# Decode attention and gated FFN, forward and backward: zero stores moved to SP, later loads to ACT, and products cut into pieces between transposes

## The chip, the cores and the metric

The kernel runs on one core of a Trainium2 chip. The metric is the device time of one launch in microseconds (us). The engines are PE (matrix products and transposes; PEld are its weight loads), DVE and ACT (vector and scalar work, and all copies out of the matrix accumulators in PSUM), POOL, and SP, which only issues transfers (DMAs). POOL issues DMAs on one queue (called software_dynamic in the profile), SP and ACT on a hardware queue each (hardware_dynamic). Each engine, and each queue's issuing engine, takes its instructions in order.

## What is computed

The reference is a forward pass and its vector-Jacobian product. Four tokens (B = 4, D = 512) are layer-normed; one branch is grouped-query attention on a cache (32 query heads, 8 K/V heads, head size 128) over the last W = 1024 of 4096 cached positions, the other a gated FFN (F = 1792):

```python
q = (xn @ wq) split into 32 heads
k, v = k_cache[:, :, Sk - W:, :], v_cache[:, :, Sk - W:, :]
p = softmax(q k^T * Dh ** -0.5);  o = p v
out = x + o @ wo + (gelu(xn @ w_gate) * (xn @ w_up)) @ w_down
```

Returned are out and the gradients of x, k_cache, v_cache, wq, wo, w_gate, w_up and w_down for a given grad_out. The gradients of the caches have the caches' full shape, (4, 8, 4096, 128) each, and are zero in the 3072 positions outside the window: these zeros have to be written too. They are 50.3 of the 112.4 MB that the kernel moves.

## The kernel before

Work goes in stages.

- The start (lines 96 to 185): layer norm, transposes of x and grad_out, masked copies `xnm` and `dym`, and a tile of zeros, `ztile`.
- The FFN stage (from 429): `hg_ps` (gate and up products), the activation, transposes of w_down (`wdT_ps`, line 492) with the `da_ps` products, then the weight gradients: `dwd_ps` (529) and `dwg_ps` (542, for gate and up), each copied by `evac` from PSUM into an output tile `osb_d` or `osb_g` and stored; then transposes of the gate and up weights (`wgT_ps`, 555), summed into `acc_ps`.
- Four groups t of two K/V heads (GP = 2, NT = 4). For each: `pre` (225) makes q and do from wq and wo (transposes `woT_ps`, products `doq_ps`); `masks` (262) makes masked copies on POOL; `scores` (271) transposes eight blocks of K (k = 0) or V (k = 1) and multiplies (`T_ps` to `T_sb`, then `S_ps`); `softmax` and `softmax_d`; `odq` (340) the products o (with V) and dq (with K); `dvdk` (364) the gradients dv and dk in 16 products each, copied into a staging tile and stored 1 MB at a time; `fin` (383) sums into out and dx (`acc_ps`, with transposes `wqT_ps`) and makes dwo (`dwo_ps`, 406) and dwq (`dwq_ps`, 418), stored from `osb_o` and `osb_q`.
- The end (592): the sums are transposed (`f_ps`), out and dx are finished and stored.

In the main loop (569) `dvdk(t, 0)`, `scores(t+1, 0)`, `dvdk(t, 1)`, `scores(t+1, 1)` and `fin(t)` follow each other as blocks. SP and POOL take their instructions in program order; PE, DVE and ACT are ordered by a scheduler. PSUM tiles of most products come from one pool of four buffers (`ps_w`), output tiles from one of three (`outp`), staging tiles from one of four. K and V tiles are one batch with two heads each, six buffers per tensor (`kvp`).

SP issues all loads, in the order FFN weights, wo and wq of group 0, K and V of group 0, wo and wq of group 1, K and V of group 1 for two batches; the later ones follow in the loop and wait for a free buffer. POOL issues all stores. The zero stores (`zeros`, 212; 32 of 1.57 MB) stand one by one between the other stores in POOL's order; the first two wait for the last load of group 0's V (line 440). `evac` (82) gives each copy out of PSUM to ACT or DVE, whichever a running sum of estimated costs favours. The memsets of `aT_b`, `dhuT_b` and `dhgT_b` (458) are on POOL.

Of the kernel before, what the change touches and what calls it, by code (L numbers as in the profile page):

```python
# [17 lines left out]
def kernel(  # L18
# [51 lines left out]
    kvp = ctx.enter_context(tc.tile_pool(name="kvp", bufs=6))  # L70
    wres = ctx.enter_context(tc.tile_pool(name="wres", bufs=2))
    attw = ctx.enter_context(tc.tile_pool(name="attw", bufs=2))
    tsb = ctx.enter_context(tc.tile_pool(name="tsb", bufs=3))
# [8 lines left out]
    def evac(out, in_, n, half=False, eng=None):  # L82

        ca, cd = (190 + n) / 1.2, (120 + (n / 2 if half else n)) / 0.96
        if eng is None:
            eng = "act" if load["act"] + ca <= load["dve"] + cd else "dve"
        load[eng] += ca if eng == "act" else cd
        if eng == "act":
            return nc.scalar.copy(out=out, in_=in_)  # L89
        return nc.vector.tensor_copy(out=out, in_=in_)  # L90
# [48 lines left out]
    acc_ps = ps_a.tile([P, 2, ND, B], FP32, name="acc_ps")  # L139

    def acc_edge(start):
        nc.tensor.matmul(acc_ps[:].rearrange("p o c b -> p (o c b)"), lhsT=ztile[0:1, 0:P],
                         rhs=ztile[0:1, 0:2 * ND * B], start=start, stop=not start)

    def acc_add(o, c, lhsT, rhs):
        nc.tensor.matmul(acc_ps[:, o, c, :], lhsT=lhsT, rhs=rhs, start=False, stop=False)  # L146

    acc_edge(True)
    S_ps = ps_a.tile([P, 2, WQ], FP32, name="S_ps")
# [41 lines left out]
    def load_w(t):  # L191
        wo_t[t] = wres.tile([P, HG, D], BF16, name="wo_sb", tag="wo")
        nc.sync.dma_start(out=wo_t[t][:], in_=wo_v[t])  # L193
        wq_t[t] = wres.tile([P, ND, CW], BF16, name="wq_sb", tag="wq")
        nc.sync.dma_start(out=wq_t[t][:], in_=wq_v[t])

    def load_kv(t, bs, which=(0, 1)):
        for i in which:
            d_, src, nm = ((k_t, A_k_cache, "kb"), (v_t, A_v_cache, "vb"))[i]
            for b in bs:  # L200
                tl = kvp.tile([P, GP, J, Dh], BF16, name=nm, tag=nm)
                ld = nc.sync.dma_start(
                    out=tl[:].rearrange("p g j d -> p g (j d)"),
                    in_=src[b, t * GP:(t + 1) * GP, K0:Sk, :].rearrange("g (m j) d -> m g (j d)", j=J))
                d_[(t, b)] = tl
        return ld
# [5 lines left out]
    def zeros(n, after=None):  # L212

        zsrc = bass.AP(tensor=ztile.tensor, offset=ztile.offset, ap=[list(ztile[:].ap[0]), [0, ZG], [1, ZW]])
        for _ in range(min(n, len(zlist))):
            og, b, g = zlist.pop(0)
            z = nc.gpsimd.dma_start(out=og[b, g:g + ZG, 0:K0, :].rearrange("g (m j) d -> m g (j d)", m=P), in_=zsrc)  # L217
            if after is not None:
                tc.add_manual_dep(z.ins, after.ins.name,
                                  mybir.DependencyInfo(mybir.DependencyClass.Sync, mybir.DependencyReason.DATA))  # L220

# [3 lines left out]
    def pre(t):  # L225
# [3 lines left out]
        for h2 in range(HG // 2):  # L229
# [6 lines left out]
            for i in range(2):  # L236
                for c in range(ND):
                    nc.tensor.matmul(dq_ps[:, 0, 2 * h2 + i, :], lhsT=woT[:, i, c, :], rhs=dyT[:, c, :],
                                     start=(c == 0), stop=(c == ND - 1))
        for h in range(HG):  # L240
# [30 lines left out]
    def scores(t, k):  # L271
# [3 lines left out]
        for b in range(B):  # L275
            for g in range(GP):
                T_ps = ps_w.tile([P, J, P], BF16, name="T_ps", tag="w")
                for j in range(J):
                    nc.tensor.transpose(T_ps[:, j, :], blks[(t, b)][:, g, j, :], ident[:])  # L279
# [3 lines left out]
                for q in range(NQ):  # L283
                    nc.tensor.matmul(S_ps[q * RG:(q + 1) * RG, k, :], lhsT=lf[:, s * RG:(s + 1) * RG],  # L284
                                     rhs=T_sb[:, q * WQ:(q + 1) * WQ],
                                     start=(s == 0), stop=(s == NS - 1), tile_position=(0, q * RG))
# [11 lines left out]
    def softmax(t):  # L298
        S = S_ps[:, 0, :]
# [24 lines left out]
    def softmax_d(t):  # L324
        E_f, rr, dP = st[t]["E"], st[t]["rr"], S_ps[:, 1, :]
# [14 lines left out]
    def odq(t, k):  # L340

        pT, blks = st[t][("PT", "dST")[k]], (v_t, k_t)[k]
        for g in range(GP):
            for j in range(J):
                q, jj = j // JQ, j % JQ
                for b in range(B):
                    c0 = q * RG + (b * GP + g) * rep
                    nc.tensor.matmul(od_ps[b * RB:b * RB + rep, k, g, :], lhsT=pT[:, jj, c0:c0 + rep],  # L348
                                     rhs=blks[(t, b)][:, g, j, :], start=(j == 0), stop=(j == J - 1),
# [6 lines left out]
        T_ps = ps_x.tile([P, GP, P], BF16, name="odT_ps", tag="x")  # L356
# [7 lines left out]
    def dvdk(t, k, stage):  # L364
        src, mr, og = ((st[t]["P"], st[t]["do"], out_3), (st[t]["dS"], st[t]["q"], out_2))[k]
        nm = ("dv", "dk")[k]
        for g in range(GP):
            stg = stage.tile([P, B, J, Dh], BF16, name="stg_" + nm, tag="stg")
            for jj in range(JQ):
                for q in range(NQ):  # L370
                    j = q * JQ + jj
                    rs = slice(q * RG, (q + 1) * RG)
                    mps = ps_w.tile([P, B, Dh], FP32, name="kv_ps", tag="w")
                    nc.tensor.matmul(mps[:].rearrange("p b d -> p (b d)"), lhsT=src[rs, jj * P:(jj + 1) * P],  # L374
                                     rhs=mr[rs, g].rearrange("p b d -> p (b d)"), start=True, stop=True,
                                     tile_position=(q * RG, 0))
                    evac(stg[:, :, j, :], mps[:], 512)
            nc.gpsimd.dma_start(  # L378
                out=og[:, t * GP + g, K0:Sk, :].rearrange("b (m j) d -> m b (j d)", j=J),
                in_=stg[:].rearrange("p b j d -> p b (j d)"))  # L380
            zeros(1)

    def fin(t):

        (o_r, oT), (dq_r, dqT) = st[t]["o"], st[t]["dq"]
        wo_sb, wq_sb = wo_t.pop(t), wq_t.pop(t)
        for h in range(HG):
            for c in range(ND):
                acc_add(0, c, wo_sb[:, h, c * P:(c + 1) * P], oT[:, h // rep, h % rep, :])
        for h2 in range(HG // 2):  # L390
# [7 lines left out]
            for i in range(2):  # L398
                h = 2 * h2 + i
                for c in range(ND):  # L400
                    acc_add(1, c, wqT[:, i, c, :], dqT[:, h // rep, h % rep, :])
        for g in range(GP):
            osb = outp.tile([P, rep, D], BF16, name="osb_o", tag="o")
            for i in range(rep):
                mps = ps_w.tile([P, D], FP32, name="dwo_ps", tag="w")
                nc.tensor.matmul(mps[:], lhsT=o_r[:, g, :], rhs=dym[:, i, :], start=True, stop=True)
                evac(osb[:, i, :], mps[:], 512)
            r0 = (t * HG + g * rep) * Dh
            nc.gpsimd.dma_start(out=out_5[r0:r0 + rep * Dh, :].rearrange("(h p) n -> p h n", p=P), in_=osb[:])  # L409
        zeros(1)  # L410
        for c2 in range(ND // 2):
            osb = outp.tile([P, 2, GP, rep, Dh], BF16, name="osb_q", tag="o")
            for ci in range(2):
                c = c2 * 2 + ci
                for i2 in range(rep // 2):
                    mps = ps_w.tile([P, 2, GP, Dh], FP32, name="dwq_ps", tag="w")
                    for i in range(2):
                        nc.tensor.matmul(mps[:, i].rearrange("p g d -> p (g d)"),
                                         lhsT=xnm[:, i2 * 2 + i, c * P:(c + 1) * P],
                                         rhs=dq_r[:].rearrange("p g d -> p (g d)"), start=True, stop=True)  # L420
                    evac(osb[:, ci, :, i2 * 2:(i2 + 1) * 2, :], mps[:].rearrange("p i g d -> p g i d"), 512)
            nc.gpsimd.dma_start(
                out=out_4[c2 * 2 * P:(c2 + 1) * 2 * P, t * CW:(t + 1) * CW].rearrange("(c p) j -> p c j", p=P),
                in_=osb[:].rearrange("p c g i d -> p c (g i d)"))
        zeros(1)
# [3 lines left out]
    with tc.tile_pool(name="ffn_w", bufs=1) as ffn_w, tc.tile_pool(name="ffn", bufs=1) as ffn:  # L429
# [6 lines left out]
        load_w(0)  # L436
        last = load_kv(0, range(B))
        load_w(1)
        load_kv(1, range(2))
        zeros(2, last)  # L440

# [14 lines left out]
        def ftb(name):  # L456
            t_ = ffn.tile([P, 4 * NF4, B], BF16, name=name)
            nc.gpsimd.memset(t_[:], 0.0)
# [49 lines left out]
        for fc in range(NF):  # L508
            for c in range(ND):
                acc_add(0, c, wd_sb[:, fc, c * P:(c + 1) * P], aT_b[:, fc, :])  # L510

        def f_rows(srcT, nm):
# [6 lines left out]
            rows = ffn.tile([P, NF4, P], BF16, name=nm)  # L519
# [3 lines left out]
        a_r = f_rows(aT_b, "a_r")  # L523
        for f4 in range(NF4):
            n = min(4, NF - 4 * f4)
            osb = outp.tile([P, 4, D], BF16, name="osb_d", tag="o")
            for i in range(n):
                mps = ps_w.tile([P, D], FP32, name="dwd_ps", tag="w")
                nc.tensor.matmul(mps[:], lhsT=a_r[:, f4, :], rhs=dym[:, i, :], start=True, stop=True)  # L529
                evac(osb[:, i, :], mps[:], 512)  # L530
            nc.gpsimd.dma_start(out=out_8[4 * f4 * P:(4 * f4 + n) * P, :].rearrange("(h p) n -> p h n", p=P),
                                in_=osb[:, 0:n, :])
            if f4 % 2:
                zeros(1)
# [119 lines left out]
```

## Time and profile before

| | us |
|---|---|
| runs of the kernel | 336.75, 338.77, 339.62 (median 338.77) |
| the profiled execution | 337.38 |
| its span, first to last instruction | 335.5 |
| PE busy in the span | 223.8 (67%) |
| DVE, ACT, POOL busy | 154.4, 127.7, 74.3 |

The mean clock granted to PE was 0.745 of full speed. The transfers moved 112.38 MB (30.93 read, 81.01 written, and a little for instructions), 335 GB/s over the span. In the page, L12 is line 12 of the kernel; `T_ps<-ident,kb` names output and inputs. "Idle before <-" tells what an engine waited for; the chain of waits goes back from the last instruction, at each step to what released it. The slices cut the span in 40 parts; a digit is the busy share in tenths.

### The profile page before, as it was taken

To read this page: it belongs to the slowest core of one execution; us is meant where nothing else is said; L and a number is where in the kernel's file an instruction comes from. 1 tells how busy PE (TensorE), PEld (TensorE's weight loads), DVE (VectorE), ACT (ScalarE), POOL (GpSimd) and SP (SyncE) were. 2 spreads that over 40 slices of the span, in tenths; PEclk is the share of its full clock that TensorE was granted. 3 is DMA by queue.
4 is the path that set the end of the run, shared out by engine and by line. 5 is a ranking of instruction groups with operands and counts; after the bars stand their busy time and mean duration, and the time that the engine had idled before them with its cause. 6 is when DMAs were issued, how large, how long until landed. Compare 5 with 4: busy or idle time off the path is not lost.

```text
span 335.5 us, 6853 instructions
## 1 busy us (share of the span) xinstructions
PE 223.8 (67%) x2956; PEld 142.8 (43%) x2956; DVE 154.4 (46%) x304; ACT 127.7 (38%) x203; POOL 74.3 (22%) x111
## 2 busy tenths in 40 slices
PE   1352182477977899698669689768959988990020
PEld 1352120164856656165346427646542664260010
DVE  6141051336553474456347454534736456870050
ACT  3012041325524363553346354334535347860010
POOL 5000212322140011070313016031201604531010
PEclk9998567559997967679956957795585879576555
DMA  5999999997900079887999999599998938999995
GB/s 175 395 361 385 373 417 418 420 417 312 411 26 2 12 259 380 352 337 301 350 415 418 416 413 410 216 358 416 417 419 347 395 149 325 376 395 403 405 389 211
DMA packets 34661, 112.38 MB, mean 335 GB/s; under 512 B 1920, under 2 KB 8072, under 8 KB 34632
## 3 DMA queue, kind: packets, MB, share of 16 engines
q0 software_dynamic: 16512, 81.01, 59.9%
q1 hardware_dynamic: 18120, 30.94, 26.3%
q8 instruction: 23, 0.38, 0.4%
q14 instruction: 6, 0.05, 0.0%
HBM read 30.93 MB, written 81.01 MB: 334 GB/s over the span
## 4 chain that ended last, share of the span: by engine, by line
PE 50%; DMA 26%; DVE 9%; ACT 5%; SPq 4%; issue 3%; POOL 1%; ACTq 0%; DVEq 0%; POOLq 0%
PE T_ps L279 13%; DMA out_dram<-osb_o 12%; PE kv_ps L374 10%; PE S_ps L284 4%; DMA wq_sb<-in_A_wq_dram 4%; DMA out_dram<-osb_g 4%; DMA vb<-in_A_v_cache_dram 3%; PE wqT_ps L395 3%; PE woT_ps L233 3%; SPq L193 3%; PE acc_ps L146 3%; DMA out_dram<-osb_d 3%; PE wgT_ps L555 3%; PE od_ps L348 3%; DVE T_sb L90 2%
## 5 line engine op out<-in xcount | busy, mean ns | idle before, releaser
L90 DVE COPY T_sb<-T_ps 128x1024 bf16<-128x1024 bf16 x40 | 27.7, 692 | 31.5 <-PE T_ps L279 31.3
L89 ACT COPY T_sb<-T_ps 128x1024 bf16<-128x1024 bf16 x24 | 24.3, 1012 | 31.2 <-PE T_ps L279 25.0
L217 POOL DMA_DIRECT2D out_dram<-ztile x32 | 22.8, 714 | 50.1 <-DMA vb<-in_A_v_cache_dram 33.1
L90 DVE CAST stg_dk<-kv_ps 128x512 bf16<-128x512 f32 x31 | 20.9, 691 | 10.4 <-PE kv_ps L374 9.8
L279 PE MATMUL T_ps<-ident,vb 128*128 128x128 bf16 x256 | 24.4, 258 | 0.0
L279 PE MATMUL T_ps<-ident,kb 128*128 128x128 bf16 x256 | 24.2, 253 | 0.0
L90 DVE CAST osb_q<-dwq_ps 128x512 bf16<-128x512 f32 x16 | 10.7, 689 | 28.3 <-DMA out_dram<-osb_o 27.7
L374 PE MATMUL kv_ps<-qmr,dS_b 32*128 32x512 bf16 x64 | 22.6, 596 | 0.3
L90 DVE CAST stg_dv<-kv_ps 128x512 bf16<-128x512 f32 x31 | 20.3, 687 | 3.2 <-PE kv_ps L374 2.7
L89 ACT CAST stg_dk<-kv_ps 128x512 bf16<-128x512 f32 x33 | 18.9, 587 | 7.1 <-PE kv_ps L374 6.7
L279 PEld LDWEIGHTS <-kb 128*128 128x128 bf16 x256 | 18.9, 115 | 5.3 <-issue 3.1
L279 PEld LDWEIGHTS <-vb 128*128 128x128 bf16 x256 | 19.4, 118 | 4.1 <-issue 1.5
L89 ACT CAST osb_q<-dwq_ps 128x512 bf16<-128x512 f32 x16 | 8.9, 588 | 30.8 <-DMA out_dram<-osb_o 30.2
L89 ACT CAST stg_dv<-kv_ps 128x512 bf16<-128x512 f32 x33 | 18.8, 587 | 3.4 <-PE kv_ps L374 3.1
L374 PE MATMUL kv_ps<-domr,P_b 32*128 32x512 bf16 x64 | 18.6, 528 | 2.1 <-DVE stg_dv L90 0.8
L233 PE MATMUL woT_ps<-ident,wo_sb 128*128 128x128 bf16 x128 | 13.0, 264 | 10.1 <-ACT osb_q L89 10.1
L378 POOL DMA_DIRECT2D out_dram<-stg_dv x8 | 6.2, 775 | 45.6 <-ACT stg_dv L89 44.0
L600 PE MATMUL f_ps<-ident_f,acc_r 128*128 128x128 f32 x8 | 2.0, 428 | 20.3 <-ACT osb_q L89 20.3
L378 POOL DMA_DIRECT2D out_dram<-stg_dk x8 | 6.2, 779 | 40.0 <-ACT stg_dk L89 28.9
L233 PEld LDWEIGHTS <-wo_sb 128*128 128x128 bf16 x128 | 10.2, 119 | 10.5 <-issue 10.3
L89 ACT CAST osb_d<-dwd_ps 128x512 bf16<-128x512 f32 x8 | 4.6, 587 | 25.4 <-PE dwd_ps L529 18.6
L409 POOL DMA_DIRECT2D out_dram<-osb_o x8 | 6.2, 771 | 36.2 <-ACT osb_o L89 34.2
(185 smaller groups left out, 420.0 us busy)
## 6 DMA issues: line engine op xcount, KB each, us to landing
out_dram<-ztile POOLq DMA_DIRECT2D x32, 1536.0 KB, 12.2
kb<-in_A_k_cache_dram SPq DMA_DIRECT2D x16, 512.0 KB, 11.1
vb<-in_A_v_cache_dram SPq DMA_DIRECT2D x16, 512.0 KB, 20.9
out_dram<-stg_dv POOLq DMA_DIRECT2D x8, 1024.0 KB, 12.1
out_dram<-stg_dk POOLq DMA_DIRECT2D x8, 1024.0 KB, 8.9
wo_sb<-in_A_wo_dram SPq DMA_DIRECT2D x4, 1024.0 KB, 22.8
wq_sb<-in_A_wq_dram SPq DMA_DIRECT2D x4, 1024.0 KB, 5.1
out_dram<-osb_o POOLq DMA_DIRECT2D x8, 512.0 KB, 9.5
```

The source lines that it names most:

```text
L89: return nc.scalar.copy(out=out, in_=in_)
L90: return nc.vector.tensor_copy(out=out, in_=in_)
L146: nc.tensor.matmul(acc_ps[:, o, c, :], lhsT=lhsT, rhs=rhs, start=False, stop=False)
L193: nc.sync.dma_start(out=wo_t[t][:], in_=wo_v[t])
L217: z = nc.gpsimd.dma_start(out=og[b, g:g + ZG, 0:K0, :].rearrange("g (m j) d -> m g (j d)", m=P), in_=zsrc)
L233: nc.tensor.transpose(wT_ps[:, i, c, :], wo_sb[:, 2 * h2 + i, c * P:(c + 1) * P], ident[:])
L279: nc.tensor.transpose(T_ps[:, j, :], blks[(t, b)][:, g, j, :], ident[:])
L284: nc.tensor.matmul(S_ps[q * RG:(q + 1) * RG, k, :], lhsT=lf[:, s * RG:(s + 1) * RG], rhs=T_sb[:, q * WQ:(q + 1) * WQ], start=(s == 0), sto ...
L348: nc.tensor.matmul(od_ps[b * RB:b * RB + rep, k, g, :], lhsT=pT[:, jj, c0:c0 + rep], rhs=blks[(t, b)][:, g, j, :], start=(j == 0), stop=(j ...
L374: nc.tensor.matmul(mps[:].rearrange("p b d -> p (b d)"), lhsT=src[rs, jj * P:(jj + 1) * P], rhs=mr[rs, g].rearrange("p b d -> p (b d)"), s ...
L378: nc.gpsimd.dma_start(out=og[:, t * GP + g, K0:Sk, :].rearrange("b (m j) d -> m b (j d)", j=J), in_=stg[:].rearrange("p b j d -> p b (j d)"))
L395: nc.tensor.transpose(wT_ps[:, i, c, :], wq_sb[:, c, h * Dh:(h + 1) * Dh], ident[:])
```

## The change

- **Zeros on SP.** `zeros()` is called once, after SP's initial loads; SP issues all 32. Each from the third on waits until the one two places before it has landed.
- **Loads.** Initial loads stay on SP; the loads for later groups (`load_next`, `load_w(t + 2, ...)`) are issued by ACT, after `odq`. K and V tiles now hold one head of four batches (1 MB, before 0.5 MB), three buffers per tensor.
- **Pieces.** The products dwd, dwg, dv, dk, dwo and dwq are put into a queue `bg`, one product with its copy per piece (dwq: two products of half width), the store at the last piece of a tile. `tick(2)` takes two pieces after each of the four steps in `pre`, the eight in `scores` and the four in `fin`; `tick(1)` one after each `wgT` step. A group puts 48 pieces in and takes 48 out; 46 come from the FFN, 14 of them taken there, so 32 are left after the last group.
- **Order.** The loop now runs all stages of a group before those of the next: `pre`, `masks`, `scores` K, `softmax`, `scores` V, `softmax_d`, `odq` twice, `fin`.
- **Sums.** The sums for out and dx are no longer kept in one PSUM tile; each part has a PSUM tile of its own (`acc_sum`, or `df_ps` in the FFN) and DVE adds it to `acc` in SBUF. K and V scores have a PSUM tile each.
- **Smaller.** Copies of bf16 transposes (`half=True`) always go to DVE; the three memsets go from POOL to DVE; the two last stores go from SP to ACT; `T_sb`'s pool and others change their buffer counts (`tsb` 3 to 5).

```diff
     def evac(out, in_, n, half=False, eng=None):
+        eng = "dve" if half else eng
...
+    def acc_add(o, ps):
+        nc.vector.tensor_tensor(out=acc[:, o], in0=ps, in1=acc[:, o], op=ALU.add)
...
+    def load_next(t, k):
+        if t + 1 < NT:
+            load_kv(t + 1, k, 1, nc.scalar)
+        if t + 2 < NT:
+            load_kv(t + 2, k, 0, nc.scalar)
...
+    def zeros():
...
+        done = []
+        for og, b, g in zlist:
+            z = nc.sync.dma_start(out=og[b, g:g + ZG, 0:K0, :].rearrange("g (m j) d -> m g (j d)", m=P), in_=zsrc)
+            if len(done) >= 2:
+                tc.add_manual_dep(z.ins, done[-2].ins.name,
...
+            done.append(z)
+    bg = deque()
+    def tick(n):
+        for _ in range(min(n, len(bg))):
+            bg.popleft()()
...
+        load_w(1, nc.sync)
+        for k in range(2):
+            load_kv(1, k, 0, nc.sync)
+        zeros()
...
-            t_ = ffn.tile([P, 4 * NF4, B], BF16, name=name)
-            nc.gpsimd.memset(t_[:], 0.0)
+            nc.vector.memset(t_[:], 0.0)
...
         for t in range(NT):
+            pre(t)
+            masks(t)
+            scores(t, 0)
+            softmax(t)
+            dvdk(t, 0)
+            scores(t, 1)
+            softmax_d(t)
+            dvdk(t, 1)
             odq(t, 0)
+            load_next(t, 1)
             odq(t, 1)
+            load_next(t, 0)
             fin(t)
             if t + 2 < NT:
+                load_w(t + 2, nc.scalar)
+            dw(t)
+        tick(len(bg))
```

`dvdk` and `dw` now only put pieces into `bg`; a piece of dv or dk is:

```python
mps = ps_w.tile([P, B, Dh], FP32, name="kv_ps", tag="w")
nc.tensor.matmul(mps[:]..., lhsT=src[rs, jj * P:(jj + 1) * P], rhs=mr[rs, g]..., start=True, stop=True, tile_position=(q * RG, 0))
evac(stg[:, :, q * JQ + jj, :], mps[:], 512)
if j == J - 1: nc.gpsimd.dma_start(out=og[...], in_=stg[...])
```

One thing follows from the program as built and not from the diff. The DMAs of SP and ACT share eight completion counters (lanes 0 to 7), given out by the framework; a DMA waits until the last user of its lane has landed. With z0 to z31 for the zeros and K(t, g), V(t, g) for the loads, the lanes tie the two engines like this (each line: the DMA that waits, what it waits for beside its own buffers; lane waits ended by an initial load, by z1 or z3, or by a load of the same group further ahead are left out):

```
SP   z7     waits for V(1,1)        ACT  V(3,0)  waits for z16
SP   z9     waits for K(1,1)        ACT  K(2,1)  waits for z18
SP   z11    waits for K(2,0)        ACT  K(3,0)  waits for z20
SP   z14    waits for wq(2)         ACT  wo(3)   waits for z22
SP   z20    waits for V(2,1)        ACT  wq(3)   waits for V(3,0)
SP   z29    waits for K(2,1)        ACT  V(3,1)  waits for z26
SP   z31    waits for K(3,0)        ACT  K(3,1)  waits for wo(3)
```

In ACT's order these issues stand among its copies: V(2,1), three osb_q and four stg_dv copies, V(3,0), two stg_dv copies, K(2,1), the copy od_r of dq, K(3,0), five stg_dv copies, wo(3), two stg_dv copies, wq(3).

## Prediction

> **What bounds the kernel now.** I read the page's slices first, then the table of waits, the chain, a table of windows, and the landing times of the zero stores.
>
> The slices: rows PE, PEclk, DMA and GB/s of the page.
>
> ```profile
> PE   1352182477977899698669689768959988990020
> PEclk9998567559997967679956957795585879576555
> DMA  5999999997900079887999999599998938999995
> GB/s 175 395 361 385 373 417 418 420 417 312 411 26 2 12 259 380 352 337 301 350 415 418 416 413 410 216 358 416 417 419 347 395 149 325 376 395 403 405 389 211
> ```
>
> A slice is 8.4 us. The DMA engines are full nearly everywhere at 350 to 420 GB/s, but empty in slices 12 to 14, just where PE works best. PE in turn is poor in slices 4 to 9. At 416 GB/s the 112.38 MB would take 270 us of the 335.5: the kernel is a transfer problem with badly placed transfers.
>
> The waits (waiter <- releaser: total, times, longest):
>
> ```profile
> PE acc_ps L146 <- DVE aT_b L474: 12.9, 1, 12.9
> DVE aT_b L474 <- POOL aT_b L458: 12.1, 1, 12.1
> POOL out_dram L217 <- DMA vb<-in_A_v_cache_dram: 33.1, 1, 33.1
> ACT osb_q L89 <- DMA out_dram<-osb_o: 30.2, 3, 20.3
> DVE osb_q L90 <- DMA out_dram<-osb_o: 27.7, 3, 19.3
> ```
>
> PE waits for a memset that stands on POOL behind a zero store held until the first V load has landed. Later ACT and DVE wait for an output buffer whose store sits on POOL's queue behind zeros. The chain (start, duration) puts those on the path:
>
> ```profile
> 50.99 9.36 DMA out_dram<-osb_d
> 60.36 8.95 DMA out_dram<-osb_g
> ...
> 159.98 9.86 DMA out_dram<-osb_o
> 218.72 8.33 DMA out_dram<-osb_o
> 299.22 22.34 DMA out_dram<-osb_o
> ```
>
> Windows (start:end, length, then PE, PEld, DVE, ACT, POOL busy, PEclk, DMA share, GB/s):
>
> ```profile
> 92.00:118.00 26.00, 20.69 (x402) 15.64 (x399) 11.91 (x29) 8.68 (x14) 3.74 (x2) 0.93 0.07 23
> 160.00:166.00 6.00, 4.67 (x106) 3.11 (x106) 2.35 (x5) 2.24 (x5) 2.94 (x4) 1.00 1.03 339
> 196.00:202.00 6.00, 6.00 (x47) 1.74 (x47) 3.71 (x6) 3.46 (x8) 1.48 (x2) 0.50 1.03 410
> ```
>
> Stages rich in loads move 339, those of stores 410 to 420. PE can be busy 6.00 of 6.00 and be granted 0.50.
>
> **The change, part by part.** All times are on the profiled execution (span 335.5, time 337.38, so 1.9 around it; the median of the runs, 338.77, is 1.4 above it).
>
> *Front.* The aT_b memset goes to DVE: the 12.9 us go. The dwd and dwg products leave the FFN stage for the queue of pieces, so the chain's 9.36 and 8.95 there go too. Worked forward: the wdT/da stage ends at 28.1 as before. Then 56 accumulation matmuls (1.6), two row sets (1.0), and the wgT stage: the chain has it from 70.0 to 88.3, of which 78.6 to 82.7 waits for a store, so 14.1. That is 44.8; I take 47 for pieces and evictions in between. Group 0 starts at 47 instead of 88.3.
>
> *Group 0.* Before, from 88.3 to the end of both od products takes 27.6 (115.9). Now 40 pieces (32 dwg, 8 dv) stand between: 32 dwg are 10.3 us of PE, or 0.32 each, so 12.8. The first od product is done 2.2 before the second, at 47 + 27.6 + 12.8 - 2.2 = 85. Fin took 9 of PE, so group 0 ends at 96.
>
> *Period of a group.* Before, woT to woT is 170.57 to 227.79, 57.2, less 8.3 waiting: 48.9. The same products are issued afterwards. For less: in 196 to 202 PE was slow at clock 0.50 on small-row products standing by themselves. For more: the softmax bubble (188.8 to 194.4) has still nothing in it. Bounds 44 and 54; I keep 48.9. By the Trainium skill (TensorE: Matmul & The Clock Gate, The HAM clock gate) activity releases the throttle, so denser PE would run at full clock. The window 196 to 202 speaks against that here: PE fully busy, 0.50. By the rule alone the 46.8 us that PE is busy from 172 to 229 (granted 0.71 to 0.85) would fall to about 35, an estimate.
>
> *Evictions and sums.* 46 bf16 evictions go from ACT (1012 ns) to DVE (692 ns): +31.8 on an engine busy 154 of 335, hidden by PE in a dense window (172 to 218: PE 39.99, DVE 24.64 of 46); if DVE became the bound, at most those 31.8. Ten adds for acc at 0.2 each hide too. POOL issues 32 DMAs fewer (0.71 each), while SP, idle before, takes them: nothing on the path. Only the stores and the masks stay on POOL. The masks stand behind a dk store whose pieces end inside pre, and are first used half a group later: 0.
>
> *Zeros and the loads: the new wait.* In the built program every DMA of SP and ACT takes one of eight completion counters and waits for that counter's last user. The counters tie zeros (z0 to z31) and later loads together: z7 waits for V(1,1) to land. On ACT, V(3,0) waits for z16, K(2,1) for z18, K(3,0) for z20, wo(3) for z22. Behind those issues, in ACT's order, stand dv evictions and the od_r copy that the dq transpose needs, so PE stops within a few instructions.
> First stop: SP's initial 16.3 MB are in by about 41, as now (same loads). z0 to z6 (1.573 MB each, 11.0) and 5.5 MB of FFN stores end near 80. V(1,1) is issued on ACT after the first od product (85), takes 5 (2.6 for 1 MB at 400 GB/s, and about 2.1 fixed: the fastest 0.5 MB store landed in 3.4), and z7 flows at 92. So the hole in the DMA stays, shortened to about 12 us.
> Second stop: until z22 has landed these must pass: z7 to z22, 25.2 MB; nine loads, 9.4; dv0, dk0, half of dv1 and four dW stores, 7.3. At 339 for the loads and 415 for the rest: 27.8 + 78.3 = 106, so z22 ends at 198. PE reaches the end of V scores of group 1 at 96 + 39.8 = 136 (170.6 to 210.4 before), when ACT issues V(3,0): ACT is held from there until 198, with some 14 us of work let through. About 48 us are lost here that the old order did not have. The zero's own pacing costs nothing if two in flight fill the engines: the fastest zero landed in 6.8, two per 6.8 are 463 GB/s, above the 415.
> The issue itself also takes ACT's time: on SP an issue took 0.37 to 0.6 when free and 10.18 when the queue was full (wo at 3.90, in the chain); ACT issues 14 loads, at 0.5 each 7 us, beside PE; I take 0 on the path, with 10 as the end if the queue fills once.
> I know no row of an ACT held by a DMA wait; the bounds are 0 (counters already full) and 60 (136 to 198, nothing let through). I take 48, since the order of the program leaves only od_r and about a dozen evictions between the four.
>
> ```profile
> DMA to landing us min/median/max: 6.8/12.2/25.5
> ```
>
> *End.* From z22 at 198: 3 us of fin(1), two groups 97.8, then 32 pieces left in the queue at 0.32 (10.2), then f_ps to the last store: 322.3 to 327.9 before (5.6) and 2.7 for issue and landing. 198 + 3 + 97.8 + 10.2 + 8.3 = 317. The old end wait of 22.34 is gone: after z22 only 33 MB remain for 119 us. Time 319 against 337.4, or 320 against the median.
>
> The Trainium skill (DMA: Bandwidth & Descriptors, Issuing engines are not separate DMA queues) says that queues of SP, ACT and POOL run on the same 16 engines, so that issuing from several saves only issue time. The rows agree on the rate, 0.97 to 1.04 busy whoever issued. By that rule alone the change would give 32 x 0.71 off POOL's path, and nothing to the time: 337. What it leaves out is order within a queue, which the rows price at 8 to 22 us a time.
>
> **Rivals.**
> *The counters hold nobody* (the zeros run ahead of the loads): compute ends at 96 + 3 x 48.9 + 18.5 = 262, and the transfers decide: 78 MB left at 92, at 400 GB/s 195, so 287, plus 4 for the last store, 295 in all. For: the zeros may take more than their part of the engines. Against: other bytes have to pass as well.
> *Slower: the zeros are thin.* If, with PE stopped and only zeros and single loads on the engines, two in flight leave gaps, z22 comes late, and 120 us of work still follow. It decides when the 42 MB take more than 128 us (z22 after 220), below 328 GB/s: that gives 342. At 305, 138 us: 352. For: load-rich windows move only 339, and a zero's fixed part (6.8 less 3.8) nearly equals its flow. Against: zeros have filled slices at 417 to 420.
> *No change that shows*: the period grows to 54 by the uncovered bubbles (+10), and z22 comes 6 later: 336.
> *The move to queues does nothing* (the rule above): 337, against it the 12.9 and the chain's rows in the front, which depend on no counter.
>
> **How the numbers follow.** Likeliest: held ACT, but a front 41 us earlier and no end wait: 320 (own range 305 to 335), chance 0.55. Counters hold nobody or little, 290 to 305: 0.11. No visible change, 335.4 to 342: 0.12. Thin zeros or another wait of ACT, over 342: 0.22. A measurement of this kernel tells about 1% from no change. Faster by over 1%: 0.66; within: 0.12; slower: 0.22. The range reaches from the first rival to the point past the decision of the second: 295 to 347.
>
> **What would show it.** Right: pre(0) starts near 47; the DMA row has a hole of one or two slices near 80 to 92 and none later before z22; ACT (as a queue) waits at the L205 load issues between 136 and 198, for zeros, with PE nearly idle and the DMA near 410; no wait for osb_o longer than a few us; the DMA thin after about 250. Wrong: if ACT waits less than 20 us there, the first rival; if the DMA stays under 340 GB/s while PE stands, the second. A group's period over 54 would refute the kept 48.9.

## The result and the profile after

| | before | after |
|---|---|---|
| median of the runs, us (before: one run more than above) | 339.19 (336.75 to 340.40) | 347.89 (347.62 to 349.19) |
| ratio, 95% interval | | 1.027 [1.021, 1.034] |
| span of the profiled execution | 335.5 | 345.6 |
| mean clock granted to PE | 0.745 | 0.696 |
| PE, DVE, ACT, POOL busy | 223.8, 154.4, 127.7, 74.3 | 228.5, 146.0, 113.6, 51.1 |

The change made the kernel 2.7% slower. The prediction was 320 us, faster, with a range of 295 to 347. Rows PE, DMA and GB/s of the page of after (a slice is now 8.6 us):

```profile
PE   1369989388968967000003798299798999597881
DMA  5999999999999997999999999999537533333384
GB/s 183 391 364 386 386 405 422 424 425 407 379 420 413 415 393 315 343 425 410 412 417 406 396 408 391 375 401 417 240 124 249 216 142 119 132 123 123 120 310 179
```

The front is what the change is for: PE is dense from slice 4 on but for one (slice 8), where before slices 4, 5, 7 and 8 stood at 1 to 4 tenths. Then come five slices (17 to 21) with PE at zero, and the DMA engines are full all through them, at 343 to 425 GB/s. So PE does not wait because transfers are thin. After slice 28 it is the reverse: PE is dense, and the DMA engines move 119 to 249 GB/s up to slice 38. The table of waits says what stood (waiter <- releaser: total, times, longest):

```profile
POOL out_dram L402 <- DMA out_dram<-ztile: 74.7, 1, 74.7
ACT osb_q L91 <- DMA out_dram<-osb_o: 55.5, 2, 53.3
DVE osb_q L92 <- DMA out_dram<-osb_o: 51.5, 2, 49.3
PE T_ps L297 <- ACT osb_q L91: 50.4, 1, 50.4
```

Read from the bottom: PE waits 50.4 us once for ACT's copy of `osb_q` (the product that it copies holds one of the four PSUM buffers from which PE's next transpose draws); ACT and DVE wait for an output buffer, that is for the store of an `osb_o`; and POOL, which issues that store, waits 74.7 us, once, for a zero store. POOL's timeline in after (start, duration, instruction, [idle before <- releaser]):

```profile
77.59 0.54 POOL L585 DMA_DIRECT2D out_dram<-osb_g  x1 [1.79 <-ACT osb_g L91]
152.86 1.51 POOL L402 DMA_DIRECT2D out_dram<-stg_dv  x2 [74.73 <-DMA out_dram<-ztile]
...
159.61 1.50 POOL L421 DMA_DIRECT2D out_dram<-osb_o  x2
```

Between 78 and 153 POOL issues nothing. What it is held at is the first dv store, line 402. In the built program this store waits for z9 and z17, zero stores of the same output tensor; the first dk store waits for z8 and z16. The two regions of the tensor do not overlap, but the framework orders these stores. Before, zeros and dv stores were on one queue, in this order anyway, and the waits of before have no row in which a dv or dk store (there line 378) waits for a zero. Now the zeros are on SP, and z17 lands at 152. Behind the held store stand, on POOL, three more dv and dk stores, group 1's masks, and the four dW stores of group 0, whose three buffers all copies of dW need. The zeros on SP had waited in their turn for loads on ACT, through the counters (SP's waits):

```profile
SPq L225 <- DMA wq_sb<-in_A_wq_dram: 9.2, 1, 9.2
SPq L225 <- DMA vb<-in_A_v_cache_dram: 7.0, 1, 7.0
```

These are z14 and z7, both ahead of z17, so the counters may have lengthened POOL's wait; by how much was not tried. The chain of waits of after (start, duration) gives the rest:

```profile
159.61 26.17 DMA out_dram<-osb_o
...
193.54 17.97 DMA vb<-in_A_v_cache_dram
211.53 10.73 ACTq L200
...
333.69 3.65 DMA out_dram<-osb_o
```

The `osb_o` store, once issued, takes 26.17 us to land, with four dv and dk stores issued in the 7 us before it; PE starts again at 186.43. Then there is a second stop that is not in the waits' upper rows: ACT is 10.73 us inside one instruction, the issue of the load of wq (line 200). The table of windows (start:end, length, then PE, PEld, DVE, ACT, POOL busy, PEclk, DMA share, GB/s):

```profile
97.00:134.00 37.00, 29.39 (x275) 17.95 (x273) 15.76 (x31) 13.85 (x27) 0.00 (x0) 0.62 0.95 387
...
160.00:186.00 26.00, 0.00 (x0) 0.00 (x0) 0.13 (x1) 0.20 (x1) 1.80 (x3) 0.50 1.02 410
...
273.00:320.00 47.00, 41.25 (x537) 26.34 (x535) 24.89 (x50) 20.89 (x41) 9.66 (x10) 0.75 0.37 135
```

POOL is at 0.00 in the first row, all of PE, DVE and ACT at nearly nothing in the second. The third shows what the stop cost: the transfers ran ahead meanwhile, and the last groups have little but PE's own work, with the DMA engines 0.37 busy.

### The profile page after: what moved, and what is told of

Its sections match the earlier page's. It is cut to its first block, busy times and chain, and to the rows that moved or that the text cites. A ratio compares the mean times of both kernels' runs of the same rounds, so it can differ in the third digit from the quotient of the medians.

```text
span 345.6 us, 6841 instructions
## 1 busy us (share of the span) xinstructions
PE 228.5 (66%) x2956; PEld 147.6 (43%) x2956; DVE 146.0 (42%) x304; ACT 113.6 (33%) x217; POOL 51.1 (15%) x76
## 2 busy tenths in 40 slices
DMA packets 34405, 112.38 MB, mean 325 GB/s; under 512 B 1664, under 2 KB 7816, under 8 KB 34376
## 4 chain that ended last, share of the span: by engine, by line
PE 28%; DMA 14%; DVE 4%; ACTq 3%; ACT 3%; issue 1%; POOL 0%; DVEq 0%
DMA out_dram<-osb_o 9%; PE T_ps L297 8%; PE kv_ps L397 6%; DMA vb<-in_A_v_cache_dram 5%; ACTq L200 3%; PE S_ps L302 3%; PE dwo_ps L417 2%; PE wqT_ps L461 2%; PE dwq_ps L431 1%; PE woT_ps L249 1%; PE acc_ps L152 1%; PE od_ps L368 1%; ACT stg_dk L91 1%; ACT stg_dv L91 1%; DVE T_sb L92 1%
## 5 line engine op out<-in xcount | busy, mean ns | idle before, releaser
L297 PE MATMUL T_ps<-ident,vb 128*128 128x128 bf16 x256 | 28.9, 258 | 50.4 <-ACT osb_q L91 50.4
L92 DVE COPY T_sb<-T_ps 128x1024 bf16<-128x1024 bf16 x64 | 44.3, 691 | 36.3 <-PE T_ps L297 35.8
L91 ACT CAST stg_dv<-kv_ps 128x512 bf16<-128x512 f32 x52 | 28.4, 589 | 29.0 <-PE kv_ps L397 28.9
L297 PE MATMUL T_ps<-ident,kb 128*128 128x128 bf16 x256 | 30.8, 267 | 0.3 <-ACT osb_g L91 0.2
L92 DVE CAST osb_q<-dwq_ps 128x512 bf16<-128x512 f32 x7 | 4.7, 687 | 51.7 <-DMA out_dram<-osb_o 51.5
L402 POOL DMA_DIRECT2D out_dram<-stg_dv x8 | 6.0, 754 | 128.5 <-DMA out_dram<-ztile 74.7
L91 ACT CAST osb_g<-dwg_ps 128x384 bf16<-128x384 f32 (+1 forms) x30 | 14.3, 537 | 15.1 <-PE dwg_ps L581 6.0
L92 DVE COPY woT<-woT_ps 128x1024 bf16<-128x1024 bf16 x16 | 11.1, 692 | 19.4 <-PE woT_ps L249 19.4
L92 DVE CAST stg_dk<-kv_ps 128x512 bf16<-128x512 f32 x18 | 12.1, 688 | 13.2 <-PE kv_ps L397 13.0
L91 ACT CAST osb_o<-dwo_ps 128x512 bf16<-128x512 f32 x23 | 12.8, 587 | 8.8 <-PE dwo_ps L417 8.2
L461 PE MATMUL wqT_ps<-ident,wq_sb 128*128 128x128 bf16 x128 | 15.6, 297 | 0.1
L92 DVE COPY wqT<-wqT_ps 128x1024 bf16<-128x1024 bf16 x16 | 11.1, 692 | 10.5 <-PE wqT_ps L461 10.5
L461 PEld LDWEIGHTS <-wq_sb 128*128 128x128 bf16 x128 | 11.7, 134 | 6.7 <-issue 6.6
```

The costliest lines, as they stand in the source:

```text
L297: nc.tensor.transpose(T_ps[:, j, :], blks[(t, g)][:, b, j, :], ident[:])
L402: nc.gpsimd.dma_start(out=og[:, t * GP + g, K0:Sk, :].rearrange("b (m j) d -> m b (j d)", j=J), in_=stg[:].rearrange("p b j d -> p b (j d)"))
L461: nc.tensor.transpose(wT_ps[:, i, c, :], wq_sb[:, c, h * Dh:(h + 1) * Dh], ident[:])
```

## The experiments

The theory, H: the dv store held on POOL for zeros on SP made the kernel slower, through what stands behind it. Rivals: ACT's loads held for zeros by the completion counters, as I had forecast (L); ACT blocked in issues because its queue is full (Q); the transfers as such (T). Each kernel starts from after, unless it says otherwise.

**The zeros in another order.** One line: the zeros of the head pair that is due first come first, so that the first dv store waits for z3 and z5 instead of z9 and z17.

```diff
-    zlist = [(og, b, g) for b in range(B) for g in range(0, G, ZG) for og in (out_2, out_3)]
+    zlist = [(og, b, g) for g in range(0, G, ZG) for b in range(B) for og in (out_2, out_3)]
```

> The changed kernel with its 32 zero stores in another order: by head pair first, then batch, so that the zeros that the first dv and dk stores are ordered behind (z17 and z16 in the changed kernel) come among the first eight. Theory H (held store): PE's 50 us idle from 136 to 186 is POOL's first dv store waiting for z17, with the osb_o stores behind it and ACT and DVE waiting for those; without it 345.6 - 50 leaves a span of 295, and the transfers (112.4 MB, full until 240 before) allow no less than about 290: span 290 to 305. Rival L (counters: ACT's loads wait for zeros): the new order loosens these waits too, so L allows a gain as well, but if ACT is still held at its load issues between 130 and 200 the span stays near 320. Rival Q (ACT's queue full at wq, 10 us twice): 335.

Measured: 312.4 us (311.34 to 313.21), 0.921 [0.915, 0.928] of before. Its waits have no row POOL <- ztile any more, and PE's 50 us stop is gone. This one line is worth 35 us and puts the change on the side where it was forecast. It is still not as low as H expected (span 309.6, expected 290 to 305). ACT's timeline shows why; its issues at line 200 and 205 (start, duration):

```profile
97.84 14.71 ACTq L200 DMA_DIRECT2D wq_sb<-in_A_wq_dram  x1
...
155.00 11.10 ACTq L205 DMA_DIRECT2D kb<-in_A_k_cache_dram  x2
...
169.40 12.49 ACTq L200 DMA_DIRECT2D wq_sb<-in_A_wq_dram  x1
```

An issue that takes 0.37 us at its shortest (the 1 MB load of wo at 168.99) takes up to 15 here, and the copies behind it on ACT wait.

**That wait alone put back.** The new zero order also moves which counters ACT's loads wait for, so the order alone does not prove H. This kernel is group_order plus one dependency:

```diff
-                    nc.gpsimd.dma_start(
+                    s_ = nc.gpsimd.dma_start(
...
+                    if t == 0 and k == 0 and g == 0:
+                        tc.add_manual_dep(s_.ins, zall[17].ins.name, mybir.DependencyInfo(mybir.DependencyClass.Sync, mybir.DependencyReason.DATA))
```

> The kernel with the zeros in the new order, and one wait put back: the first dv store of group 0 waits for the eighteenth zero (z17). Nothing else is edited. H: POOL is held again from about 78 to 150, PE idle about 50 us, span 340 to 350. L by itself: no wait of POOL matters, span as with the new order alone. Q: as with the new order alone.

Measured: 347.01 us (345.34 to 347.60), 1.022 [1.015, 1.028]: all that was gained is lost again. Its waits:

```profile
POOL out_dram L404 <- DMA out_dram<-ztile: 74.0, 1, 74.0
ACT osb_q L91 <- DMA out_dram<-osb_o: 55.6, 2, 53.4
PE T_ps L299 <- ACT osb_q L91: 50.0, 1, 50.0
```

They repeat those of after to within a microsecond. One wait on one store, with what stands behind it, costs 347.0 - 312.4 = 34.6 us: H stands.

**The forecast wait alone.** group_order, with the four loads on ACT made to wait for the zeros that the prediction named:

```diff
+    after_z = {("V", 3, 0): 16, ("K", 2, 1): 18, ("K", 3, 0): 20, ("wo", 3): 22}
+
+    def behind(ld, key):
+        if key in after_z:
+            tc.add_manual_dep(ld.ins, zall[after_z[key]].ins.name, mybir.DependencyInfo(mybir.DependencyClass.Sync, mybir.DependencyReason.DATA))
```

> The kernel with the zeros in the new order, and ACT's loads V(3,0), K(2,1), K(3,0) and wo(3) made to wait for z16, z18, z20 and z22, as the counters did in the changed kernel; no store waits for a late zero. The scheduler sees these waits and puts the loads later in ACT's order. The prediction's step (L): ACT held for some 48 us, span 320 to 340. H: the waits cost at most what K(2,1) comes late for the scores of group 2, 0 to 20 over the new order alone.

Measured: 317.61 us (one run), 5.2 above group_order. The wait exists and stops PE once:

```profile
PE T_ps L306 <- DMA kb<-in_A_k_cache_dram: 21.2, 1, 21.2
```

The scheduler puts the held loads behind copies that are ready, in ACT's order, so that PE goes on and stops only for the data itself. Of the 21 us, 16 do not show in the time; one place where they come back is the blocked issues, since wq's second issue takes 0.38 us here and 12.49 in group_order (the first takes 15.73 here). So loads that come late for these zeros cost about 5 us. ACT held in front of copies that are ready, which is how I had come to 48, does not occur here, and was not tried by itself.

**No zeros at all.** The zero stores are left out of after.

```diff
-        for og, b, g in zlist:
+        for og, b, g in zlist[:0]:
```

> The changed kernel without any zero store (50.3 MB are not written, so the cache gradients outside the window are left out). H and L both: what remains is the compute path, 262 by the prediction's sum; with Q's two full queues up to 20 more where the loads still fill ACT's queue: 262 to 285.

Measured: 280.76 us (one run, span 279.0). `pre` starts at 42.4, 93.9, 149.8 and 204.1, so a group takes 51.5, 55.9 and 54.3 us with no zero about. ACT's wq issues, which took 14.71 and 12.49 in group_order, are here:

```profile
92.57 1.78 ACTq L200 DMA_DIRECT2D wq_sb<-in_A_wq_dram  x1
...
149.21 2.04 ACTq L200 DMA_DIRECT2D wq_sb<-in_A_wq_dram  x1
```

So the loads that ACT issues do not block it by themselves; they do when they drain beside the zeros. The time lies in the expected range, but not for the reason named there: ACT's issues are short, and what is above 262 lies in the length of the groups.

**Zeros in portions; weights on SP; K on SP too.** Three steps from group_order. The first puts the zeros on SP eight at a time, after each group's loads, and is the control for the second, which gives the later wo and wq loads to SP, where only zeros stand behind them. The third gives it the later K loads as well.

```diff
-        zeros()
+        zeros(8)
...
             if t + 2 < NT:
-                load_w(t + 2, nc.scalar)
+                load_w(t + 2, nc.sync)
+            zeros(8)
```

```diff
-            load_kv(t + 1, k, 1, nc.scalar)
+            load_kv(t + 1, k, 1, (nc.sync, nc.scalar)[k])
...
-            load_kv(t + 2, k, 0, nc.scalar)
+            load_kv(t + 2, k, 0, (nc.sync, nc.scalar)[k])
```

> Control for the next run: group_order with the 32 zero stores put on SP in portions of 8 per group and not all at the start, everything else the same (all later loads still on ACT). Theory Q (ACT blocked at an issue because ITS OWN hardware queue is full, 14.7 + 11.1 + 12.5 us in group_order): nothing about that queue changes while zeros run, so issues of 10 to 15 us stay and the time is 308 to 316. Rival Z (the blocking comes from the rate at which zeros take the transfer engines): portions end the zeros of a group and give the loads room now and then, ACT's long issues shrink below 5 us each, 290 to 305.

> As portions, and the weight loads wo(2), wq(2), wo(3), wq(3) go to SP (in program order, behind the zeros of the group before) and no longer to ACT. Theory Q: ACT's issues of 10 to 15 us at the wq load are gone (SP may be blocked there, which holds only zeros back), some 25 to 38 us of ACT's time come free, of which the part on the chain (14.7 and 10.6 in group_order's chain) comes off: 290 to 303. Theory T (transfers bound group_order up to 242 us at about 400 GB/s, so that ACT's blocking stands in the place of a wait for data): less than 5 us comes off, 307 to 315, and PE waits for kb, vb or wq_sb instead.

> weights_on_SP with the later K loads also on SP (their buffers come free only after odq, so SP waits for that, and the zeros and weight loads behind it too); ACT keeps the V loads alone. Theory Q: the last issues of several us on ACT (7.8 and 5.3 at the K loads) go: up to 8 us off, 288 to 296. Rival T: the kernel is now bound by the transfers (112.38 MB at 405 GB/s are 277 us, and some 10 us at the start move less), nothing to gain: 295 to 300. Against both: SP held at a K load lets the transfers run dry, over 302.

Measured: portions 316.42 (one run); weights_on_SP 297.75 (294.59 to 299.28), 0.876 [0.870, 0.883]; K_and_weights_on_SP 292.68 (292.53 to 293.29), 0.862 [0.860, 0.865]. ACT's long issues in portions:

```profile
97.44 14.82 ACTq L200 DMA_DIRECT2D wq_sb<-in_A_wq_dram  x1
...
169.04 14.31 ACTq L200 DMA_DIRECT2D wq_sb<-in_A_wq_dram  x1
```

and in weights_on_SP:

```profile
86.00 7.83 ACTq L205 DMA_DIRECT2D kb<-in_A_k_cache_dram  x2
...
143.61 5.29 ACTq L205 DMA_DIRECT2D kb<-in_A_k_cache_dram  x2
```

Portions gain nothing by themselves. With the weight loads off ACT the 14 us issues go, and 18.7 us with them (against portions); with K off too, the 7.8 and 5.3 go, and another 5.1. Of the two theories Q is borne out, and T is refuted up to there; that ACT is blocked because its queue is full remains an inference, since no row shows a queue's fill. The window from 92 to 142, where ACT is blocked in group_order, first in group_order and then in weights_on_SP:

```profile
92.00:142.00 50.00, 32.98 (x315) 20.38 (x315) 17.59 (x34) 15.65 (x32) 8.20 (x8) 0.57 1.02 409
...
92.00:142.00 50.00, 42.49 (x482) 26.84 (x486) 25.52 (x50) 22.64 (x43) 8.99 (x9) 0.67 1.03 409
```

Both kernels move the same 409 GB/s, but PE is busy 32.98 of 50 us in the one and 42.49 in the other: what was missing was not bandwidth. K_and_weights_on_SP is near T's bound; its DMA row and its window from 142 to 192:

```profile
DMA  5999999999999999999999999999999999999992
```

```profile
142.00:192.00 50.00, 43.22 (x417) 26.94 (x416) 22.91 (x43) 20.21 (x39) 9.62 (x10) 0.58 1.03 405
```

Every slice but the first and the last is at least 0.9 busy, and 112.38 MB at 405 GB/s are 277 of its 291.6 us. It beats both kernels of this study, before by 46.8 us.

**One zero in flight instead of two,** from group_order:

```diff
-            if len(done) >= 2:
-                tc.add_manual_dep(z.ins, done[-2].ins.name,
+            if len(done) >= 1:
+                tc.add_manual_dep(z.ins, done[-1].ins.name,
```

> group_order with one zero store in flight on SP instead of two. Theory T: zeros take a smaller share of the transfers up to 242 us, loads come sooner, zeros are spread over the last 70 us, where group_order moves only 250 GB/s: 290 to 305, with the granted bandwidth near 380 to the end. Theory Q as well, since ACT's queue drains faster: issues at wq below 8 us. Rival: the dv and dk stores of each group wait for zeros that now come later (first dv store behind z5), POOL stops again and with it the copies: over 315.

Measured: 330.32 us (329.43 to 331.29), 0.975 [0.969, 0.980]: the rival named there. The zeros come later, and so do the dv stores ordered behind them. Its waits, and then its chain:

```profile
POOL out_dram L402 <- DMA out_dram<-ztile: 76.3, 2, 43.3
ACT osb_q L91 <- DMA out_dram<-osb_o: 40.0, 3, 23.0
```

```profile
168.60 5.08 DMA out_dram<-ztile
...
301.91 18.71 DMA out_dram<-osb_o
```

The zeros are now 79% of the chain, one after the other from 38.85 to 298; the last of them lets the last dv stores go, and the `osb_o` store behind these. The fastest take 5.1 us, 1.573 MB at 308 GB/s. In slices 26 to 30 of its page the DMA engines are 0.5 to 0.8 busy, at 241 to 303 GB/s. So one in flight leaves gaps; no row shows two in flight with nothing beside them. ACT's second wq issue took 2.41 us instead of 12.49, as Q has it, but the first still took 9.29 (14.71 in group_order), above the 8 that Q had set.

**dW stores on ACT.** The changed kernel with its zero order kept; lines 421 and 436 issue from ACT, so that only dv, dk and masks stand behind the held store.

```diff
-                nc.gpsimd.dma_start(out=out_5[r0:r0 + rep * Dh, :].rearrange("(h p) n -> p h n", p=P),
+                nc.scalar.dma_start(out=out_5[r0:r0 + rep * Dh, :].rearrange("(h p) n -> p h n", p=P),
...
-                nc.gpsimd.dma_start(
+                nc.scalar.dma_start(
```

> The changed kernel, its zero order kept, with only the stores of osb_o and osb_q issued by ACT and not by POOL, so that they no longer stand behind the first dv store, which is still held for the 18th zero (POOL's wait at L402 stays near 75 us). Theory H (the held store hurts through what stands behind it on POOL): the 53 us waits of ACT and DVE for osb_o go; PE runs on until the four staging tiles are used up, which are held as well, some 16 pieces or 8 transposes steps (10 to 15 us) later, so the stop of 50 us shrinks to 25 to 40 and the time is 322 to 340. If the stop came from the loads or from zeros as such, it stays near 50 and the time at 345 to 350. Doubt: ACT's queue takes 8.4 MB more, and its issues may be blocked for another 10 us.

Measured: 343.27 us (one run), above H's 322 to 340. The step that H names happened: the first dv store is held as before, the waits for `osb_o` are down to 3.1 us at the longest, and the next thing that is held takes their place, the staging buffers of dv.

```profile
POOL out_dram L402 <- DMA out_dram<-ztile: 77.6, 1, 77.6
...
ACT stg_dv L91 <- DMA out_dram<-stg_dv: 32.3, 1, 32.3
```

PE stopped for 22.9 us up to 160.7, and 6.1 more from 163 on, 29 against 50, and group 2's `pre` started at 188.6, not 209.2. But ACT's queue now had the stores too, and the gain went into one issue:

```profile
194.20 18.36 ACTq L200 DMA_DIRECT2D wq_sb<-in_A_wq_dram  x1
```

Group 3 started at 264.5, 8 before after's 272.6, and the end is 4.2 earlier (spans 341.4 and 345.6). A stop shortened in one queue was given back in the next one.

**Before, with the memsets on DVE alone** (line 458 of the kernel before):

```diff
-            nc.gpsimd.memset(t_[:], 0.0)
+            nc.vector.memset(t_[:], 0.0)
```

> The kernel before with one part of the change alone: the three memsets of the FFN's padded tiles on DVE and no longer on POOL behind the zero stores. My sum put 12.9 us of the front end on that wait. If it was on the path that sets the end: 322 to 330 and the first od product about 12 us sooner. If the work behind it waits for data anyway (loads and zeros share the transfers): within 3 us of 338.

Measured: 339.01 us (one run), before 338.41. The 12.9 us wait is gone, and the row sets start at 19.40 instead of 42.52. But group 0 starts at 88.09, before at 87.72: the copies of dwd now wait for the three output buffers, and PE's products behind them, since the stores of these buffers stand on POOL behind the same zero.

```profile
PE dwg_ps L542 <- ACT osb_d L89: 20.6, 1, 20.6
...
DVE osb_d L90 <- DMA out_dram<-osb_d: 21.0, 1, 21.0
```

The gain of the front in after (87.7 to 42.6) is that of the queues and pieces together; the memsets alone gave none of it.

## Why the prediction was wrong

- **Front and group 0: right.** `pre(0)` starts at 42.6 (I took 47), the first od product is done at 83.7 (85), group 1 starts at 95.9 (96). That the last is so close is in part luck: group 0 began 4.4 us earlier than I had it and took 53.2 instead of 49.
- **The first stop, a hole in the DMA near 80 to 92: wrong.** Slices 10 to 12 of after, 78 to 104 us, moved 407, 379 and 420 GB/s: no hole. The wait itself came as forecast, z7 went out at 91.09 (I had 92), but ACT's loads, issued from 82.36 on, and the last zeros before z7 kept the engines busy meanwhile.
- **The failed step: "nothing on the path. Only the stores and the masks stay on POOL."** I followed the counter waits of SP's and ACT's issues in the built program, and not the waits of the stores that stay on POOL. The first of them waits for z17: POOL was held for 74.7 us, PE stopped for 50, and this wait alone, put back into group_order, cost 34.6 us, where the prediction has nothing. The question that I asked of ACT, what stands behind a held issue, would have led, put to POOL, to the buffers of `osb_o` and the stop. Of the signs that the prediction names it is "no wait for osb_o longer than a few us" that failed: ACT's longest was 53.3.
- **The second stop: its length right by luck, its cause wrong.** Forecast was ACT held from 136 to 198, with about 48 us lost; measured was PE stopped from 136 to 186, but by POOL. ACT issued V(3,0) at 193.54, as soon as it got there: while PE stood, the zeros had run past all the numbers that the counters asked for (z24, which waits for z22, went out at 180.77; I had z22 at 198). Loads that wait for these zeros cost 5 us where the scheduler knew of the wait (loads_behind_zeros); what ACT held in front of ready copies would have cost stays open.
- **After the stop: 28 us more than the sum.** I had 3 us of group 1 left after the release and then two groups. Measured, `pre(2)` starts at 209.2 (201 by the sum), then 14.4 pass until its transposes go on at 223.57, most of them in the 10.73 us issue of wq. From there to group 3 it is 49.0 (48.9); from group 3 to `f_ps` 65.5 (59.1); and 7.5 to the end (8.3): 8.2 + 14.4 + 0.1 + 6.4 - 0.8 = 28.3, and 317.3 (the sum unrounded) + 28.3 = 345.6, the span.
- **ACT's issues: mis-sized.** I took 0 with 10 as the end, "if the queue fills once". ACT was blocked twice in after (10.2 and 10.7), and for 38 us in all in group_order. Moving the loads off ACT gave back 18.7 and 5.1.
- **The group's period: only partly right.** 48.9 matches the stretch from 223.57 (49.0), which leaves a group's start out. From `pre` to `pre` it is 51.5 to 55.9 without zeros, and two of three are above the 54 that I named as the bound. My sum of the compute work, 262, was 279 in no_zeros. Which of the uncovered bubbles make up the 17 us was not tried.
- **Rivals.** "The zeros are thin" is refuted as a cause of after: 410 GB/s while PE stands still. "The counters hold nobody", 295, is near what the change becomes when both POOL and ACT are nearly free of held issues: 297.8 and 292.7. In the changed kernel itself the counters did hold SP, for 7.0 and 9.2 us above. "Moving the queues does nothing" is refuted in both directions.
- **Slips without weight.** 96 + 3 x 48.9 + 18.5 is 261, not 262; by the prediction's own terms some 36 MB remain after z22, not 33; in the empty slices 12 to 14 of before PE stands at 7, 7 and 8 tenths, not at its best, and slice 6 of its poor stretch at 8; and the zero on POOL was held for the last load of group 0's V, not the first.

Two pages were weighed in the prediction. The Trainium skill (DMA: Bandwidth & Descriptors, Issuing engines are not separate DMA queues) says that queues share the engines and that issuing from several saves only issue time, usually small beside the transfer itself. The runs agree on the rate, the same 409 GB/s whoever issued the weights, but the issue time was not small: up to 14.71 us for a 1 MB load of wq in group_order, where these loads took 46.5 us to land (the median of two), and which queue holds the loads was worth 24 us in all. The Trainium skill (TensorE: Matmul & The Clock Gate, The HAM clock gate) says that activity releases the throttle. The window of K_and_weights_on_SP above speaks against it as a forecast: PE busy 43.22 of 50, granted 0.58. In no_zeros, with 42.95 busy in the same window, 0.69 was granted:

```profile
142.00:192.00 50.00, 42.95 (x475) 26.25 (x473) 25.76 (x48) 22.52 (x43) 9.71 (x10) 0.69 0.62 232
```

## What to carry to other kernels

When a stream of transfers goes from one queue to another, list for every issue that stays behind what it now waits for across queues, in the built program, and then what stands behind it on its engine: here a store whose data were ready held the stores behind it, three buffers, two copying engines and PE. Order the stream by who is ordered behind it; one line did that here and was worth 35 us. And give loads to an engine that has nothing else to do: an issue that took 10 to 18 us here held the copies behind it on the same engine as well.

## What the runs showed of the hardware

- An issue on a hardware queue can hold its engine for many us; that the queue is then full is inferred. On ACT the 1 MB load of wq took 1.78 and 2.04 us to issue with no zeros, 9.29 and 2.41 with one zero in flight, 10.19 and 10.73 (after) or 14.71 and 12.49 (group_order) with two, and 18.36 once ACT's queue had stores as well. The shortest issues of 1 MB took 0.37.
- The same engine busy for as long can be granted very different clocks: 0.58 and 0.69 in the two windows of 142 to 192 named above, with PE busy 43.22 and 42.95 of 50 us. The DMA engines were 1.03 busy in the first and 0.62 in the second. Which property of the work or of the transfers beside it sets the clock was not settled.
